# Raw loads interleaved with weight pairs, weight passes moved into a unit's levels, six copies for eight, and a second queue for two units' x

## The chip, the cores and the metric

The kernel runs on one core of a Trainium2 chip. The metric is device time in microseconds. Inputs and outputs lie in HBM. The five engines are PE (TensorE), DVE (VectorE), ACT (ScalarE), POOL (GpSimd) and SP (SyncE), which issues most of the DMAs.

## The reference

An attention-like recurrence over 768 tokens, for 4 batches of 8 heads of 48 columns, and then an MLP over the 3072 tokens:

```python
f = 1.0 / (1.0 + np.exp(-f_logit))
for t in range(S):
    state = f[:, :, t, :, None] * state + np.einsum('bhd,bhe->bhde', k[:, :, t], v[:, :, t])
    y[:, :, t] = np.einsum('bhd,bhde->bhe', q[:, :, t], state)
x = y.transpose(0, 2, 1, 3).reshape(B * S, H * D)      # 3072 x 384
h = x @ w_in                                           # 384 x 2048
out = (h * (1.0 / (1.0 + np.exp(-1.702 * h)))) @ w_out # 2048 x 384
```

The weights are given as 64-bit floats, the rest as 32-bit floats.

## The kernel before

**Units.** The tokens are cut into 12 units of 256 (`NALL`), three to a batch. A unit's attention (`attention(n)`) is a list of parts. First, f, q and k are loaded raw (`load_raw`, three tensors j = 0, 1, 2 for f, q, k) and turned so that the head's columns lie on partitions (`turn`: on PE for units 0 and 1, on DVE's stream transpose, L354, from unit 2 on). Then six levels of a scan follow. At each level the products of f over a stretch (`tot`, POOL, L425) are multiplied into X, which holds q and k (`promote`, DVE, L528 or L532), half of X is set aside on ACT (`set_aside`: Kc, L503, and Qc, L509), PE forms scores (`score`, L434), and DVE and ACT move them from PSUM to the matrix A (`evacuate`, L475, L494, L484). In units 2 and on, two levels share one score tile, `sc`, of which there is one. A later tile of it waits until the earlier one has been moved to A. A and v give y (`add`, L543), k and v give the chunk states (L652, DVE L676/L677), and states and q are added into y (L698).

**From y to x.** Part "W" copies y from PSUM to `yT` on ACT (L712: for each head of a pair, two directions f and two groups g, 48 partitions x 256 elements, so eight copies a unit), and `to_x` moves `yT` to `xT` in six DMAs, three a head (L762 the large one, L767 the two rests). Unit 11 has its own copy of this, `whole`.

**MLP.** `xT` is what the MLP multiplies: h = x w_in in blocks of 128 columns (`mlp_h`, L1110; three matmuls a block) and o = g w_out (`mlp_o`, L1124), for units 0 and 1 block by block as the weights come in. From unit 2 on it uses products of sums of the weights (L878, L1016).

**Weights.** The 64-bit weights come in 16 pairs of blocks of 128 (`pairs`: for each four blocks two of w_in, then two of w_out). A pair is fetched by SP into one of three buffers `bits` (`fetch_weights`, L208; two DMAs for w_in, one for w_out). It is then turned into 32-bit floats: a pass on ACT (L239) and three on DVE (L235, L228, and the add at L238). `convert()` emits the next of the three DVE operations, and the ACT pass with the first. When a pair is done, `fetch_weights` issues the next fetch. So where `convert()` stands in the program also decides where the next fetch stands in SP's queue. Pair 4, 5, 8, 9, 12 and 13 are w_in's for blocks 4 to 7, 8 to 11 and 12 to 15; 6, 7, 10, 11, 14 and 15 are w_out's.

**Order.** Up to the end of unit 2's attention the order on each engine is that of the program text (`manual_schedule`). `opening()` emits unit 0; `follow(n, fill, plan)` emits the parts of units 1 and 2. After each part it emits so many MLP items (`fill`), so many `convert()` and so many other operations (`chores`), by the table `PLAN`. An MLP item waits in the list until the pairs that it needs have been emitted. `parts_of(n)` lists a unit's parts, with the turns of unit n+1 (`begin_f`, `begin`, `begin_k`, `begin_gates`) between them, and with the loads of the raw tensors, each of which has one buffer. SP, ACT, DVE and PE each work their list in order.

In before, unit 1's second part issues all three raw loads of unit 2, and unit 2's turns each issue the raw load of unit 3 right behind them:

```python
second = parts[1][1]
parts[1] = parts[1][0], lambda: (second(), [load_raw(n + 1, j) for j in range(3)])
```

Of the kernel before, what the change touches and what calls it, by code (L numbers as in the profile page):

```python
# [23 lines left out]
def kernel(  # L24
# [33 lines left out]
    nc = tc.nc  # L58
# [6 lines left out]
    U = 256  # L65
# [190 lines left out]
            fetch_weights()  # L256


    def load_raw(n, j, engines=(nc.sync,)):
        if n >= NALL:  # L260
            return
        b, s0 = n // NU, n % NU * U
        src = (f_logit, q, k)[j]
        first = s0 - (j == 1)

        def span(head, token, dims, d=0):
            return bass.AP(src.tensor, src.offset + ((b * H + head) * S + token) * D + d, dims)
        if n < N_FILL:
            for a in range(NP):
                engine = engines[a * len(engines) // NP]  # L270
                to = by_pair[j][32 * a:32 * (a + 1), :, :R * D]
                if first < 0 and a == 0:

                    for r, rows in ((1, 16), (17, 15)):
                        engine.dma_start(
                            out=to[r:r + rows], in_=span(0, r * R - 1, [[R * D, rows], [S * D, 2], [1, R * D]])
                        )
                    engine.dma_start(out=to[:1, :, D:], in_=span(0, 0, [[R * D, 1], [S * D, 2], [1, (R - 1) * D]]))
                else:
                    engine.dma_start(out=to, in_=span(2 * a, first, [[R * D, 32], [S * D, 2], [1, R * D]]))  # L280
            return
        for f in (1, 0):
            for r in range(4):
                lo = 32 * (r % 2)
                width = R4 * D - lo
                part = span(r // 2, first + (0 if f else HALF), [[R4 * D, 32], [2 * S * D, NP], [1, width]], lo)
                nc.sync.dma_start(out=by_half[32 * r:32 * (r + 1), j, f, :, :width], in_=part)  # L287
            if f and first < 0:
                for r in range(4):
                    lo = 32 * (r % 2)  # L290
                    nc.sync.dma_start(
                        out=by_half[32 * r:32 * r + 1, j, f, :, :D - lo],
                        in_=q[b - 1, r // 2::2, S - 1:S, lo:].rearrange("a t d -> t a d"),
                    )
# [25 lines left out]
    def rows(h):  # L320
        return slice(h * HS, h * HS + D)
# [6 lines left out]
    def attention(n):  # L328
# [58 lines left out]
        def begin_f(pieces=None):  # L387
            def decay():
                turn(0, lambda f: F[:, ORDER.index(f) * SLOT:(ORDER.index(f) + 1) * SLOT], sigmoid, pieces)
            if n > N_FILL + 1 and "moved" in copied:  # L390
                with tc.issue_after(copied["moved"].ins):
                    decay()
            else:
                decay()
            if n >= N_FILL:
                load_raw(n + 1, 0)

        def begin():
            turn(1, lambda f: slot(query(n, f)))
            if n >= N_FILL or (n == 1 and 1 == 0):  # L400
                load_raw(n + 1, 1)

        def begin_k(between=None):
            turn(2, lambda f: slot((KR, KF)[f]))
            if n >= N_FILL or (n == 1 and 2 == 0):
                load_raw(n + 1, 2)
            if n >= N_FILL:
                set_aside(0, True)
                rest = between and between()
                promote(0)  # L410
                if rest:
                    rest()
            else:
                set_aside(0)
# [34 lines left out]
        def columns(h, g):  # L449

            return rows(h ^ g)
# [84 lines left out]
        def add():  # L536


            t["py"] = ps.tile([P, NG, NP, 2, HS], F32, tag="y", name=f"y_{n}")
            for a in range(NP):  # L540
                for f in (1, 0):
                    for h, g in TILES:
                        nc.tensor.matmul(  # L543
                            t["py"][columns(h, g), g, a, f, :],
                            lhsT=vts[n][g * HS:(g + 1) * HS, f, (2 * a + h) * D:(2 * a + h + 1) * D],
                            rhs=A[g * HS:(g + 1) * HS, h * NP + a, f, :],
                            start=(f == 1 and a == 0), stop=False, skip_group_check=True,
                        )
# [9 lines left out]
        def levels(l):  # L558

            scores()  # L560
            score(0, l, queries_aside(l))
            score(1, l + 1, queries(l + 1))
            promote(l + 1, l + 2 < NL)
            if l + 2 < NL:
                promote(l + 2)
            evacuate(l, l + 1)
            if l == 2:
                reverse_v(n)
# [71 lines left out]
        def _():  # L640
# [17 lines left out]
            if not n:  # L658
# [2 lines left out]

                seen = t["py"][HS:HS + 1, 1, 0, 1, :1]
                nc.scalar.copy(seen, seen)
            load_v(n + 1)
            st = att.tile([P, NC, NP, D], F32, tag="st", name=f"st_{n}", bufs=2)
            D64 = t["tms"][NL].rearrange("p (f a g) -> p f g a", f=2, a=NP)
            prev = t["ahead"] = last.get("st")
# [13 lines left out]
        def _():  # L681
# [24 lines left out]
            xT = mlp.tile([P, NK, width(n)], F32, tag="xT", name=f"xT_{n}", bufs=3)  # L706

            def half(h):
                for f in (1, 0):
                    for g in range(NG):  # L710
                        at, step = (g * HS, 1) if f else (U - 1 - g * HS, -1)
                        nc.scalar.copy(view(yT[rows(h)], at, [[U, NP], [step, HS]]), py[columns(h, g), g, :, f, :])  # L712
                to_x(lambda h: (yT[rows(h), :NK], lambda r, d: yT[r:r + d, NK]), xT[:, :, :U], NG, (h,))
            half(0)
            if n > N_FILL and n < NALL - 1:
                xTs[n] = xT
# [38 lines left out]
            xTs[n] = xT  # L755
            sums_of_x(n)

        def to_x(y, x, ng, hs=range(2)):

            for h in hs:  # L760
                most, rest = y(h)
                nc.sync.dma_start(out=x[h * D:(h + 1) * D].rearrange("p c (g t) -> p c g t", g=ng), in_=most)  # L762
                at = 0
                while at < D:
                    c, p = (h * D + at) // DR, (h * D + at) % DR
                    w = min(D - at, DR - p)
                    nc.sync.dma_start(  # L767
                        out=x[D2 + p:D2 + p + w, c].rearrange("p (g t) -> p g t", g=ng), in_=rest(h * HS + at, w)
                    )
                    at += w  # L770
# [419 lines left out]
    def parts_of(n):  # L1190

        parts = list(units[n][1])
        _, inter = parts.pop()
        if n and n != N_FILL:
            kind, scores = parts[0]
            _, ahead = units[n - 1][1][-1]
            def both():
                rest = ahead()
                scores()
                if rest:  # L1200
                    rest()
            parts[0] = kind, both
        if n + 1 < NALL:
            begin_f, begin, begin_k, begin_gates = units[n + 1][0]
            i = len(parts)
            if n + 1 < N_FILL:

                parts.append(("K", lambda: (begin_k(), begin_gates())))
                kind, head = parts[0]
                parts[0] = kind, lambda: (head(), load_raw(n + 1, 1), keep_up(1))  # L1210
                parts.insert(4, ("B", lambda: (begin(), load_raw(n + 1, 2))))
                parts.insert(2, ("B", begin_f))
            else:
                kind, states = parts.pop()
                if n in CARRY:
                    parts += [("B", begin_f), ("B2", begin), ("S1", lambda: (states(), begin_gates())), ("K3", begin_k)]
                elif n < N_FILL:
                    second = parts[1][1]
                    parts[1] = parts[1][0], lambda: (second(), [load_raw(n + 1, j) for j in range(3)])
                    def own():  # L1220
                        rest = inter()
                        rest()
                    parts += [(kind, states), ("W", own), ("B", begin_f), ("B", begin), ("B", lambda: (begin_gates(), begin_k()))]
                else:
                    parts += [("B", begin_k), (kind, lambda: (states(), begin_gates()))]
                    parts.insert(i - 3, ("B", lambda: (begin_f(), begin())))
        else:
            parts.append(("W", inter))
        return parts
# [53 lines left out]
    def opening():  # L1283
# [44 lines left out]
        for _ in range(NOP):  # L1328
# [4 lines left out]
    WAITS = {(1, "W", 1): 3}  # L1333
    PLAN = {
# [4 lines left out]
    }  # L1339
    fill += mlp_blocks((0, 0)) + mlp_blocks((0, 1))  # L1340
    fill += mlp_blocks((1, 0), (1, 1)) + mlp_blocks((0, 2), (1, 2)) + mlp_blocks((0, 3), (1, 3))
# [53 lines left out]
```

## Time and profile before

| | us |
|---|---|
| median of 3 runs (596.13 to 596.91) | 596.39 |
| the profiled execution | 596.8 |
| its span | 595.0 |
| PE busy | 568.3 (96%) |
| DVE busy | 435.8 (73%) |
| ACT busy | 299.6 (50%) |
| POOL busy | 136.2 (23%) |
| mean granted TensorE clock | 0.991 |

The span is what the profile covers; the profiled execution's own time is 1.8 us longer. All times inside a profile count from the span's start. In a line of a time line, the first number is the start, the second the time from the first to the last of the merged instructions, then engine, line, operation, output and inputs, the shape and the number of instructions; the bracket tells how long the engine was idle before it and which instruction ended that. PE shows each 32-bit matmul as two passes, so an h block of three matmuls is "x6" and an o matmul is "x2". SPq and ACTq are DMA issues on the queues of SP and ACT. The table by windows gives the busy time of each engine, then the granted TensorE clock, the busy share of the DMA engines and GB/s.

### The profile page before, as it was taken

The page shows a single profiled execution, that of the slowest core. Times are in us where ns is not written, and L with a number is a line of the kernel's source. Part 1 is how long each engine was busy: PE and PEld are TensorE (multiplying, and loading weights), DVE is VectorE, ACT ScalarE, POOL GpSimd, SP SyncE. Part 2 cuts the span into 40 slices and gives each one's busy share as a digit, 9 for nine tenths or more (in the row PEclk, how much of TensorE's full clock was granted, in tenths as well). Part 3 has the DMA queues.
Part 4 walks back from the last instruction along what each step waited for, and adds up shares of the span by engine and source line. Part 5 has one row for each costly group of instructions (what it writes and reads, how often), then busy time and mean ns, then how long its engine had stood idle before and what let it go on. Part 6 is the DMA issues. An engine that isn't in the chain of part 4 may idle for free.

```text
span 595.0 us, 18527 instructions
## 1 busy us (share of the span) xinstructions
PE 568.3 (96%) x7832; PEld 517.2 (87%) x7832; DVE 435.8 (73%) x697; ACT 299.6 (50%) x610; POOL 136.2 (23%) x226
## 2 busy tenths in 40 slices
PE   7989887899999999999999999999999999999997
PEld 6756574667789999999999999999999999998896
DVE  2897568985979778798787797786887786461284
ACT  4765534324452575474474574563663564552440
POOL 3020020145226610610600700700600602203000
PEclk9989899999999999999999999999999999999999
DMA  6868977434452443343452243453352121001000
GB/s 181 192 164 200 225 193 173 134 78 95 122 143 66 128 107 84 94 123 92 120 141 55 76 115 88 123 139 63 96 146 55 45 55 29 29 2 27 28 1 28
DMA packets 86772, 60.34 MB, mean 101 GB/s; under 512 B 33505, under 2 KB 78465, under 8 KB 86689
## 3 DMA queue, kind: packets, MB, share of 16 engines
q1 hardware_dynamic: 86352, 58.76, 39.4%
q8 instruction: 62, 1.02, 0.7%
q10 hardware_dynamic: 337, 0.39, 0.3%
q14 instruction: 21, 0.17, 0.1%
HBM read 45.49 MB, written 8.91 MB: 91 GB/s over the span
## 4 chain that ended last, share of the span: by engine, by line
PE 79%; DVE 8%; DMA 5%; issue 3%; ACT 2%; SPq 2%; DVEq 0%; ACTq 0%
PE h L1016 16%; PE o_Y L878 13%; PE o_Z L878 9%; PE h L1110 9%; PE h_y L1016 6%; PE sc L434 5%; PE o_X L878 5%; PE o L1124 4%; PE o_W L878 4%; DMA bits<-in_moe_w_in_dram 3%; PE y L698 2%; PE y L543 2%; PE sc L652 2%; DMA raw<-in_f_logit_dram 2%; SPq L287 1%
## 5 line engine op out<-in xcount | busy, mean ns | idle before, releaser
L532 DVE TENSOR_TENSOR X<-X,tot 128x1024 f32<-128x1024 f32 x50 | 65.6, 1313 | 42.7 <-PE sc L434 36.4
L503 ACT COPY Kc<-X 128x512 f32<-128x512 f32 x72 | 48.3, 670 | 71.6 <-DVE X L532 59.9
L978 POOL TENSOR_TENSOR E<-xT 128x128 f32<-128x128 f32 (+1 forms) x36 | 18.6, 528 | 235.0 <-DMA xT<-yT 204.4
L1110 PE MATMUL h<-xT,w_in 128*128 128x256 f32 x288 | 66.9, 388 | 4.8 <-DVE w_in L238 2.5
L1110 PEld LDWEIGHTS h<-xT,w_in 128*128 128x128 f32 x288 | 54.9, 193 | 15.1 <-issue 3.4
L1016 PE MATMUL h<-E,w_in 128*128 128x128 f32 (+1 forms) x476 | 62.5, 277 | 0.3 <-DVE g L1044 0.3
L1016 PEld LDWEIGHTS h<-E,w_in 128*128 128x128 f32 x476 | 57.3, 192 | 1.0 <-issue 0.5
L878 PE MATMUL o_Y<-T,S 128*128 128x192 f32 x320 | 57.6, 329 | 0.0
L1046 ACT ACTIVATE g<-g 128x512 f32<-128x512 f32 (+1 forms) x70 | 40.4, 590 | 26.6 <-DVE g L1044 26.6
L878 PEld LDWEIGHTS o_Y<-T,S 128*128 128x128 f32 x320 | 52.3, 190 | 0.5
L1044 DVE TENSOR_TENSOR g<-g,h 128x512 f32<-128x512 f32 (+1 forms) x58 | 36.1, 638 | 15.1 <-PE h L1016 14.1
L712 ACT COPY yT<-y 48x256 f32<-48x256 f32 x88 | 32.3, 367 | 28.8 <-PE y L698 27.8
L1124 PE MATMUL o<-w_out,g 128*128 128x384 f32 x128 | 45.4, 503 | 0.1
L354 DVE STREAM_TRANSPOSE X<-raw 128x512 f32<-128x512 f32 x40 | 42.3, 1116 | 3.1 <-PE y L698 2.7
L494 DVE COPY_PREDICATED A<-masks,sc 128x256 f32<-128x256 uint32 (+1 forms) x98 | 42.0, 504 | 0.0
L1124 PEld LDWEIGHTS o<-w_out,g 128*128 128x128 f32 x128 | 24.2, 195 | 15.5 <-issue 1.9
L1035 ACT ACTIVATE g<-h 128x512 f32<-128x512 f32 (+1 forms) x52 | 28.5, 576 | 10.0 <-PE h L1016 9.7
L1114 ACT ACTIVATE g<-h 128x256 f32<-128x256 f32 x48 | 17.8, 384 | 30.4 <-PE h L1110 30.3
L434 PE MATMUL sc<-X,Kc 48*64 48x64 f32 x1344 | 28.4, 221 | 3.8 <-ACT Kc L503 2.2
L434 PEld LDWEIGHTS sc<-X,Kc 48*64 48x64 f32 x1344 | 24.2, 135 | 8.0 <-ACT Kc L503 4.2
L878 PE MATMUL o_X<-w_out,g 128*128 128x192 f32 x160 | 29.9, 332 | 0.5 <-ACT o_X L842 0.5
L878 PE MATMUL o_W<-T,g 128*128 128x192 f32 x160 | 29.5, 331 | 0.0
(161 smaller groups left out, 1171.4 us busy)
## 6 DMA issues: line engine op xcount, KB each, us to landing
bits<-in_moe_w_out_dram SPq DMA_DIRECT2D x8, 768.0 KB, 5.4
raw<-in_f_logit_dram SPq DMA_DIRECT2D x48, 96.0 KB, 2.4
raw<-in_k_dram SPq DMA_DIRECT2D x48, 96.0 KB, 3.3
bits<-in_moe_w_in_dram SPq DMA_DIRECT2D x8, 576.0 KB, 6.7
raw<-in_q_dram SPq DMA_DIRECT2D x44, 96.0 KB, 2.2
k_tok<-z SPq DMA_DIRECT2D x64, 64.0 KB, 1.7
kt<-k_tok SPq DMA_DIRECT2D x16, 256.0 KB, 3.4
out_dram<-osb SPq DMA_DIRECT2D x20, 192.0 KB, 1.9
```

Source lines behind the costliest of these rows:

```text
L354: nc.vector.transpose(view(out, at, [[HALF, NP], [step, R4], [R4 * step, 32]]), by_half[:, j, f].rearrange("p a (j d) -> p (a j) d", j=R4) ...
L434: nc.tensor.matmul(t["sc"][h][g * HS:(g + 1) * HS, a, s, :], lhsT=t["Kc", l][rows(h), x:x + HS], rhs=rhs(h, a, g), start=True, stop=True,)
L494: moved = nc.vector.copy_predicated(out=view(A, c * HALF + at, dims), mask=mask.bitcast(U32), data=got)
L503: nc.scalar.copy(c.rearrange("p (n two m) -> p n two m", two=2, m=m), view(X, KF * SLOT, [[2 * m, SLOT // (2 * m)], [(KR - KF) * SLOT + m, ...
L532: nc.vector.tensor_tensor(x, x, y, ALU.mult)
L712: nc.scalar.copy(view(yT[rows(h)], at, [[U, NP], [step, HS]]), py[columns(h, g), g, :, f, :])
L878: nc.tensor.matmul(t[name], lhsT=lhs(f), rhs=rhs(f), start=(new and i == 0), stop=(i == HF - 1), skip_group_check=True,)
L1016: nc.tensor.matmul(ph[:, t], lhsT=WA[a][:, f * P:(f + 1) * P], rhs=E[n][b], start=(root and t == 0), stop=not goes_on, skip_group_check=True,)
L1044: nc.vector.tensor_tensor(to, to, part, ALU.add if sign > 0 else ALU.subtract)
L1046: nc.scalar.activation(to, to, AF.Gelu_apprx_sigmoid)
L1110: nc.tensor.matmul(ph, lhsT=w_in[:, c, ff * P:(ff + 1) * P], rhs=xTs[n][:, c, :], start=(c == 0), stop=(c == NK - 1))
L1124: nc.tensor.matmul(t["po"], lhsT=g[ff // FG][:, ff % FG, tt * P:(tt + 1) * P], rhs=w_out[:, ff, :], start=(ff == ffs[0]), stop=(ff == ffs[ ...
```

## The change

- Raw loads of unit 2: f behind unit 1's second part as before, q behind its fourth, k behind its fifth. Pair 6 thereby stands between f and q on SP, and pair 7 between q and k.
- Raw loads of unit 3: no longer behind unit 2's turns but in unit 2's own parts: f ahead of the second part, q behind it, k behind the third. The fetches of pairs 12, 13 and 14 stand ahead of all of them on SP, that of pair 15 between f and q.
- v of unit 2 is loaded by a later part (`begin`) of unit 1.
- `HOLES`: seven `convert()` are emitted inside unit 2's levels: three between setting aside level 0 and its multiplication, two, one and one ahead of later ones. `PLAN` emits fewer elsewhere and other numbers of MLP items in unit 1.
- In `half`, one copy over 112 partitions takes both heads of group 0; group 1 is copied as before. That makes four copies in the first half, two in the second. So that the 16 partitions between the heads hold something, `add` multiplies with 64 columns of v rather than 48 for the first head of group 0. Unit 11 keeps eight copies.
- For units 0 and 1, the three DMAs of the second head's x are issued by ACT, SP and ACT in turn, not by SP alone.

```diff
+    HOLES = {(N_FILL, 0): 3, (N_FILL, 1): 2, (N_FILL, 2): 1, (N_FILL, 4): 1}
+    def convert_in(n, l):
+        for _ in range(HOLES.get((n, l), 0)):
+            convert()
...
             if n >= N_FILL:
                 set_aside(0, True)
                 rest = between and between()
+                convert_in(n, 0)
                 promote(0)
...
+                        to, w = (slice(0, HS), HS) if h == g == 0 else (columns(h, g), D)
                         nc.tensor.matmul(
-                            t["py"][columns(h, g), g, a, f, :],
-                            lhsT=vts[n][g * HS:(g + 1) * HS, f, (2 * a + h) * D:(2 * a + h + 1) * D],
+                            t["py"][to, g, a, f, :],
+                            lhsT=vts[n][g * HS:(g + 1) * HS, f, (2 * a + h) * D:(2 * a + h) * D + w],
...
             score(1, l + 1, queries(l + 1))
+            convert_in(n, l + 1)
             promote(l + 1, l + 2 < NL)
             if l + 2 < NL:
+                convert_in(n, l + 2)
                 promote(l + 2)
...
-            load_v(n + 1)
+            if n != N_FILL - 1:
+                load_v(n + 1)
...
             def half(h):
-                for f in (1, 0):
-                    for g in range(NG):
+                for g in range(h, NG):
+                    for f in (1, 0):
                         at, step = (g * HS, 1) if f else (U - 1 - g * HS, -1)
-                        nc.scalar.copy(view(yT[rows(h)], at, [[U, NP], [step, HS]]), py[columns(h, g), g, :, f, :])
-                to_x(lambda h: (yT[rows(h), :NK], lambda r, d: yT[r:r + d, NK]), xT[:, :, :U], NG, (h,))
+                        to, of = (rows(h), columns(h, g)) if g else (slice(0, HS + D),) * 2
+                        nc.scalar.copy(view(yT[to], at, [[U, NP], [step, HS]]), py[of, g, :, f, :])
+                two = (nc.scalar, nc.sync) if h and n < N_FILL else (nc.sync,)
+                to_x(lambda h: (yT[rows(h), :NK], lambda r, d: yT[r:r + d, NK]), xT[:, :, :U], NG, (h,), two)
...
                 elif n < N_FILL:
-                    second = parts[1][1]
-                    parts[1] = parts[1][0], lambda: (second(), [load_raw(n + 1, j) for j in range(3)])
+                    def followed(i, *loads):
+                        kind, fn = parts[i]
+                        parts[i] = kind, lambda: (fn(), [load() for load in loads])
+                    for i, j in ((1, 0), (3, 1), (4, 2)):
+                        followed(i, lambda j=j: load_raw(n + 1, j))
...
-                    parts += [(kind, states), ("W", own), ("B", begin_f), ("B", begin), ("B", lambda: (begin_gates(), begin_k()))]
+                    parts += [(kind, states), ("W", own), ("B", begin_f), ("B", lambda: (begin(), load_v(n + 1))), ("B", lambda: (begin_gates(), begin_k()))]
                 else:
...
+                    second, third = parts[1][1], parts[2][1]
+                    parts[1] = parts[1][0], lambda: (load_raw(n + 1, 0), second(), load_raw(n + 1, 1))
+                    parts[2] = parts[2][0], lambda: (third(), load_raw(n + 1, 2))
...
-        1: ((0, 6, 2), (1, 1, 13), (2, 3, 0), (8, 4, 6), (16, 0, 11), (7, 0, 0), (0, 4, 0), (1, 0, 5), (6, 2, 0), (8, 6, 6),
+        1: ((0, 6, 2), (1, 1, 13), (2, 3, 0), (8, 4, 6), (3, 2, 0), (0, 0, 0), (0, 2, 0), (1, 2, 0), (1, 3, 0), (8, 4, 0),
             (3, 0, 1), (3, 0, 0), (2, 0, 0)),
-        2: ((8, 6, 0), (6, 7, 1), (14, 4, 0), (0, 0, 3), (5, 1, 10), (11, 2, 0), (0, 1, 6), (7, 6, 3)),
+        2: ((8, 2, 0), (6, 3, 1), (14, 6, 0), (0, 0, 3), (5, 0, 10), (11, 0, 0), (0, 0, 6), (7, 0, 3)),
```

More of the change, by code (lines that the diff above doesn't have):

```diff
@@ L394, in begin_f @@
                 decay()
-            if n >= N_FILL:
+            if n > N_FILL:
                 load_raw(n + 1, 0)
@@ L399, in begin @@
             turn(1, lambda f: slot(query(n, f)))
-            if n >= N_FILL or (n == 1 and 1 == 0):
+            if n > N_FILL:
                 load_raw(n + 1, 1)
@@ L404, in begin_k @@
             turn(2, lambda f: slot((KR, KF)[f]))
-            if n >= N_FILL or (n == 1 and 2 == 0):
+            if n > N_FILL:
                 load_raw(n + 1, 2)
@@ L756, in whole, with to_x @@
             sums_of_x(n)
-        def to_x(y, x, ng, hs=range(2)):
+        def to_x(y, x, ng, hs=range(2), queues=(nc.sync,)):
             for h in hs:
                 most, rest = y(h)
-                nc.sync.dma_start(out=x[h * D:(h + 1) * D].rearrange("p c (g t) -> p c g t", g=ng), in_=most)
+                engines = [queues[i % len(queues)] for i in range(3)]
+                engines.pop(0).dma_start(out=x[h * D:(h + 1) * D].rearrange("p c (g t) -> p c g t", g=ng), in_=most)
                 at = 0
@@ L766, in to_x @@
                     w = min(D - at, DR - p)
-                    nc.sync.dma_start(
+                    engines.pop(0).dma_start(
                         out=x[D2 + p:D2 + p + w, c].rearrange("p (g t) -> p g t", g=ng), in_=rest(h * HS + at, w)
```

## The prediction

> **What bounds the kernel now.** I read the page first, then PE's time line, SP's issue time line and the chain of waits. The page says that PE is busy for 568.3 of 595.0 us, and shows where the rest is.
>
> ```profile
> PE   7989887899999999999999999999999999999997
> PEclk9989899999999999999999999999999999999999
> ```
>
> Slices are 14.9 us. From slice 8 (119 us) on PE is full, so a microsecond won ahead of that point reaches the end if nothing behind it gives it back. All edits but one act ahead of 160 us. PE's time line shows what is lost there:
>
> ```profile
> 63.19 0.68 PE L652 MATMUL sc<-vt,kn 64*64 64x48 f32 x32 [1.37 <-ACT kn L605]
> 64.86 2.82 PE L1110 MATMUL h<-xT,w_in 128*128 128x256 f32 x6 [0.99 <-issue]
> ...
> 76.04 9.30 PE L1110 MATMUL h<-xT,w_in 128*128 128x256 f32 x42 [1.30 <-issue]
> ...
> 101.86 0.69 PE L434 MATMUL sc<-Qc,Kc 48*64 48x64 f32 x32 [3.42 <-DVE A L494]
> ...
> 108.98 10.22 PE L1110 MATMUL h<-xT,w_in 128*128 128x256 f32 x46 [1.77 <-DVE w_in L238]
> ```
>
> The last bracket is the idle time before the line and what ended it. I add up the work between 56.32 and 108.98 at full pace: h 1.33 us a block of three matmuls (10.22 for 46 passes), o 0.665 a matmul (6.65 for 20 passes), sc 1.09 a pair of levels, tkn 1.1, both y 1.04, sc of the states 0.93. That gives 37.7 us; the stage takes 52.7. So 15 us is the most that this stage can return. The chain of waits names a cause at both ends of it:
>
> ```profile
> 56.68 5.06 DMA bits<-in_moe_w_out_dram
> 61.76 0.90 ACT bits L239
> 62.66 0.48 ACT kn L605
> ...
> 98.35 7.60 DMA bits<-in_moe_w_in_dram
> ```
>
> Weight pairs land late because SP's single queue sends three blocks of raw loads ahead of them:
>
> ```profile
> 40.51 7.18 SPq L287 DMA_DIRECT2D raw<-in_f_logit_dram  x8
> 47.82 4.59 SPq L287 DMA_DIRECT2D raw<-in_q_dram  x8
> 52.52 4.07 SPq L287 DMA_DIRECT2D raw<-in_k_dram  x8
> 56.68 0.90 SPq L208 DMA_DIRECT2D bits<-in_moe_w_out_dram  x2
> ```
>
> The same is seen again at 77.09 to 96.85 (raw of unit 3) ahead of pairs 12 and 13, whose second one lands at 105.95. PE's h at 108.98 waits for pair 13's conversion (108.92).
>
> **Part 1: unit 2's raw loads, pairs 6 and 7 between them.** SP's order becomes f, pair 6, q, pair 7, k, pairs 8, 9, 10, then xT. It reaches f about 0.85 us sooner, since two of xT's six DMAs leave it (0.6 each in L762/L767's rows). Pair 6 is issued at 47.0, behind f. A w_out pair takes 5.4 us to land (page part 6), up to 7.8 in the rows of bits; I take 6.2, since f lies ahead: 53.2. Q's last DMA needs pair 6's queue slot (each SP transfer waits for the one eight before it in the instruction list), so pair 7 goes at 54.2 and lands at 59.6; k's last needs that slot, so pair 8 goes at 60.0 and lands at 66 (w_in: 6.5 to 6.7). Level 5's chain does not suffer: pair 6 is wanted on ACT at 54.
>
> What is queued behind the new waits counts more. ACT now holds, in this order, both kn copies, pair 7's pass, one gelu, pair 8's pass, one gelu, the yT copies. The kn copies are free at 57.5, so the 1.37 us stall goes; pair 5's last pass on DVE moves ahead of level 5's multiplications, which wait for PE (57.09), so the 0.75 us wait at 58.79 goes. But yT now waits for pair 8: 66.0 + 0.90 (pass) + 0.7 (gelu and dispatch) = 67.6, against 69.21 before. PE reaches that point near 64 and waits. Gain in yT: 1.6 us.
>
> **Part 2: six copies, two queues.** Copies cost 0.38 each (3.03 for 8, at 48 rows; a row of 112 partitions is not in the trace. I take the same time for the same 256 elements a row; the dearest neighbour, twice as long, would eat the gain). Before: 69.21 to h's start at 76.04 is 6.83. After: six copies 2.3, then ACT's own issue and landing of the 48x768 DMA (73.28 to 76.04 before: 2.76) makes 5.1, so h of unit 1 starts at 72.7, 3.3 us sooner. Two issues on ACT cost 0.43 to 0.69 each in ACT's queue rows of the opening; they delay pair 9's pass, which F's and X's transposes follow on DVE (end 80.0, before 82.31), so they are covered. In unit 0 they push Kc at 36.05 by 0.45 us; xT is there 1.8 sooner; nothing of this survives, as pairs 6 to 8 gate what follows. The 64-column weight loads add nothing: 64 passes already move 64 columns each in 1.04.
>
> The Trainium skill (DMA: Bandwidth & Descriptors, "Issuing engines are not separate DMA queues") says that transfers started by several engines share the same 16 DMA engines, and only issue time is saved. By that rule the second queue is worth one issue, 0.6, and the start would be the same 72.7 here, as I count no bandwidth; if pair 10's bytes still fill the engines, it would be about 74.
>
> **Part 3: passes in holes.** Unit 2's block: eight h blocks 72.7 to 83.3 (h_7 now ahead of sc), then sc. Kc_0 follows the gelu of h_5 (80.7): 81.1 to 82.5 with Qc. In before, X's multiplication followed at once (84.56 behind 84.48). Now pair 10's pass on ACT (0.90), its shift (0.55) and its add (0.95) come between, as X's line stands behind them on DVE: +2.4. So X runs 85.05 to 86.3, Kc_1 to 87.0; the second half of sc waits on PE from 84.0 to 87.0, 3.0 us against 0.57. This hole is not hidden; it is the dearest piece of the change. Next level: pair 11's pass and shift put X at 89.1, Qc_2 ends 91.6, X 92.9, A's three rows (0.68 + 1.31) 94.9. PE's o blocks end at 93.0, so sc_18 waits till 94.9; before, 93.21. So far the whole gain is lost (-1.7).
>
> Then it turns. Before, six passes stood on DVE between 92.87 and 96.63, and sc_19 waited 3.42 for A. After, X starts at 96.05, one add, Kc/Qc, X to 99.85, A to 101.15: sc_19 at 101.2 (before 101.86). Behind it pair 13 landed long ago (issued at 84, once pair 10's buffer is free, landing near 90): shuffle 0.58, two passes 1.1, a sum 0.5, add 0.96: 104.2. PE arrives at 104.05 after 4 o and 2 h passes. So h goes on at 104.2 against 108.98: **-4.8**.
>
> **Behind that.** DVE holds the same work after this point in both programs; T's sums now come before F's transposes, and pair 15's shift waits for its ACT pass at 115. I find slack left: st ends at 138 where PE wants it at 141; sc_22 has about 1 us. Unit 3's raw q and k are issued later (97 to 106), needed at 119 and 127. I charge 0.3 of those bounds (0 to 1.5). Eight later units save two copies, 0.75 us of ACT each; PE's waits there are 1.9 us on DVE's g in all, so 0 to -1, taken -0.2.
>
> Sum: profiled time 596.8 (span 595.0 and 1.8 around it) - 4.8 + 0.3 - 0.2 = 592.1. That execution is 0.4 above the median of 596.39; I give 592.
>
> **Rivals.** The instruction lists of both programs show every edit in place, so that it does not happen is none. (a) *Slower: pair 8 holds yT.* Pairs 6, 7 and 8 land one after another through the slots of q and k. With 7.8 us each (the longest row) instead of 5.4 to 6.6, they land at 54.8, 63.0 and 71.5; yT starts at 73.1, h at 78.2, and the walk above ends at 109.7: +0.7, and with one more long PE wait in it about +2.5: 599. It decides from a landing of 70.8 on. For it: eight slots, SP waiting 4.0 + 2.9 us for bits in this stage; against it: 307 GB/s moved at 60 to 66.
> (b) *Given back.* The holes' 3.0 and 1.9 us come in full and sc_19 has no gain, because DVE's T sums or pair 15 make PE wait: 596, no change.
> (c) *More.* The holes' X lines start at the transposes' end (80.0) as the gelus run ahead, and the later stalls shrink: 589.
> (d) *The clock.* In before, the 3.42 us of idle time is followed by a low granted clock:
>
> ```profile
> 100.00:102.00 2.00, 0.14 (x9) 0.17 (x12) 2.00 (x7) 1.00 (x2) 0.00 (x0) 1.00 1.05 239
> 102.00:104.00 2.00, 2.00 (x65) 1.62 (x64) 1.66 (x4) 0.93 (x1) 0.00 (x0) 0.64 1.04 263
> 104.00:106.00 2.00, 2.00 (x5) 1.04 (x4) 1.38 (x2) 0.00 (x0) 0.00 (x0) 0.51 1.04 271
> ```
>
> The clock is the third number from the end; about 3.4 us at half pace cost 1.7. The 1.30 and 1.77 us waits had no such tail. Mine of 3.0 may have it: at 88 it is hidden, since o would then end at 94.7, before 94.9. If it comes after sc_18 it adds 1.7: 593.8. The Trainium skill (TensorE: Matmul & The Clock Gate, Part 1) says that an idle window of about 3.4 us halves the clock, in free-running windows. The trace agrees in size.
>
> **Numbers.** Forecast with (d)'s two outcomes 0.62 (590 to 594.5), (c) 0.10, (b) 0.11, (a) 0.17. A measurement of this kernel tells about 0.2% (1.2 us) from no change: faster means under 595.2, slower over 597.6. Faster 0.72, same 0.11, slower 0.17. The range leaves out most of (a) and the far end of (c): 589 to 597.4.
>
> **What would show it.** Right: kn with no DMA wait ahead of it; unit 1's h start between 72 and 74; a PE wait of about 3 us before the second half of sc of unit 2; none over 1 us at h of blocks 8 to 11; pair 13 landed by 95. Wrong: yT starting after 70 behind pair 8, X's first multiplication at once behind Qc_0, or new PE waits between 110 and 160.

## The result, and the profile after

| | before | after |
|---|---|---|
| median of 20 runs each, us | 597.04 (596.13 to 600.37) | 594.91 (592.77 to 597.54) |
| ratio after/before, 95% interval | | 0.9955 (0.9943 to 0.9967) |
| the profiled execution, us | 596.8 | 595.5 |
| its span | 595.0 | 593.2 |
| PE busy | 568.3 | 568.8 |
| ACT busy | 299.6 | 288.4 |
| mean granted TensorE clock | 0.991 | 0.991 |

The change makes the kernel faster by 0.45%, 2.7 us by the ratio (the medians differ by 2.1 us). The forecast was 592.0 us, with a range of 589 to 597.4, so sign and range held. The gain was about half of the 4.4 us forecast by the medians and three fifths by the ratio, and 594.9 lies just outside the 590 to 594.5 that had the chance of 0.62. In the two profiled executions the difference is 1.3 us, where the sum of the prediction had 4.7.

The page of after, for the two rows that were read first in before:

```profile
PE   7979888999999999999999999999999999999997
PEclk9989988999999999999999999999999999999999
```

PE is full from slice 7 on (before: slice 8). The clock row has its 8s in slices 2, 5 and 6 (before: 2 and 4); slice 5 is 74 to 89 us. PE's time line of after for the same stage:

```profile
61.71 1.12 PE L663 MATMUL sc<-vt,kn 64*64 64x48 f32 x64
63.18 1.45 PE L1125 MATMUL h<-xT,w_in 128*128 128x256 f32 x6 [0.35 <-issue]
...
73.51 0.70 PE L1125 MATMUL h<-xT,w_in 128*128 128x256 f32 x2 [1.49 <-DMA xT<-yT]
74.42 11.88 PE L1125 MATMUL h<-xT,w_in 128*128 128x256 f32 x46 [0.21 <-DVE w_in L238]
...
89.71 0.70 PE L442 MATMUL sc<-X,Kc 48*64 48x64 f32 x32 [2.78 <-ACT Kc L511]
...
97.34 0.70 PE L442 MATMUL sc<-Qc,Kc 48*64 48x64 f32 x32 [1.57 <-DVE A L502]
...
98.43 5.83 PE L1139 MATMUL o<-w_out,g 128*128 128x384 f32 x12
104.19 0.70 PE L442 MATMUL sc<-Qc,Kc 48*64 48x64 f32 x32
...
106.67 10.52 PE L1125 MATMUL h<-xT,w_in 128*128 128x256 f32 x48
```

Three of the waits shown of before are gone: 1.37 us for kn, 3.42 us for A and 1.77 us for the weights. Unit 1's h starts at 73.51 instead of 76.04. In their place stand 2.78 us for Kc, in the first hole, and 1.57 us for A. Two lines are too long for their work: 46 passes of h take 11.88 us (10.22 in before), and 12 of o take 5.83 us (4.14 in before). The table by windows says why; the clock is the third number from the end:

```profile
74.00:76.00 2.00, 1.79 (x5) 1.30 (x5) 2.00 (x4) 0.00 (x0) 0.00 (x0) 0.67 0.88 324
76.00:78.00 2.00, 2.00 (x6) 1.54 (x5) 2.00 (x3) 1.15 (x2) 0.00 (x0) 0.50 1.06 310
...
98.00:100.00 2.00, 2.00 (x38) 1.33 (x30) 1.41 (x3) 0.06 (x1) 0.00 (x0) 0.64 0.78 116
100.00:102.00 2.00, 2.00 (x4) 1.09 (x4) 1.55 (x2) 1.08 (x2) 0.00 (x0) 0.51 0.98 379
```

The clock is at half (0.50) from 74.7 to 78.1 and from 98.6 to 102.0, and once more from 37.1 to 40.5. The profiled execution of before has as many such stretches (37.7 to 41.1, 65.0 to 68.4, 102.6 to 106.0), so the mean clock is 0.991 in both. They don't all cost the same. In before, the one at 102.6 lies ahead of the 1.77 us for pair 13, and the chain of waits comes to pair 13 by DVE and SP, not by PE, so it cost nothing. What the one at 65.0 cost is not shown: an h block took 2.82 us in it (1.45 in after), y stands behind that block, and yT's first copy waits for y:

```profile
69.21 3.03 ACT L712 COPY yT<-y 48x256 f32<-48x256 f32 x8 [0.31 <-PE y L698]
```

In after, the one at 74.7 lies ahead of the chain of holes. The two profiled executions also hide a difference. Over all runs the mean clock is 0.990 in before (the 71 runs beside the experiments) and 0.994 in the full change (26 runs), so the change has about one stretch fewer as a rule.

The gain along the way, at points with the same work done ahead of them: 1.9 us at the third pass of h of block 8 (107.10 against 108.98), 2.0 us at 128.23 against 130.24, and 1.3 us at the last o_Z (587.12 against 588.40). The spans differ by 1.8 us, but the time around the span grew from 1.8 to 2.2 us, in every run of after (2.14 to 2.30), so the last matmul is the better mark.

### The profile page after: what moved, and what is told of

The parts are those of the page before. It is cut to its first block, busy times and chain, and to the rows that moved or that the text cites. A ratio compares the mean times of both kernels' runs of the same rounds, so it can differ in the third digit from the quotient of the medians.

```text
span 593.2 us, 18507 instructions
## 1 busy us (share of the span) xinstructions
PE 568.8 (96%) x7832; PEld 518.0 (87%) x7832; DVE 438.1 (74%) x697; ACT 288.4 (49%) x588; POOL 139.2 (23%) x226
## 4 chain that ended last, share of the span: by engine, by line
PE 83%; DVE 6%; ACT 5%; DMA 3%; issue 2%; ACTq 1%; SPq 0%; DVEq 0%
PE h L1031 16%; PE o_Y L893 13%; PE h L1125 10%; PE o_Z L893 9%; PE sc L442 6%; PE h_y L1031 6%; PE o L1139 6%; PE o_X L893 5%; PE o_W L893 4%; DMA bits<-in_moe_w_in_dram 2%; PE y L710 2%; PE y L552 2%; PE sc L663 2%; DVE X L540 1%; DVE g L1059 1%
## 5 line engine op out<-in xcount | busy, mean ns | idle before, releaser
L540 DVE TENSOR_TENSOR X<-X,tot 128x1024 f32<-128x1024 f32 x50 | 67.6, 1351 | 39.7 <-PE sc L442 31.4
L993 POOL TENSOR_TENSOR E<-xT 128x128 f32<-128x128 f32 (+1 forms) x36 | 16.0, 453 | 227.3 <-DMA xT<-yT 227.3
L725 ACT COPY yT<-y 48x256 f32<-48x256 f32 (+1 forms) x66 | 21.1, 369 | 29.2 <-PE y L710 28.8
L388 POOL TENSOR_SCALAR F<-F 128x1024 f32<-128x1024 f32 x10 | 12.9, 1286 | 81.0 <-ACT F L391 81.0
```

The costliest lines, as they stand in the source:

```text
L540: nc.vector.tensor_tensor(x, x, y, ALU.mult)
```

## The experiments

All were timed in five rounds beside runs of the kernel before, four kernels to a comparison, with six to twelve runs of each. Medians of before were 597.63, 598.1 and 597.9 us in the three comparisons, so ratios are compared, not times.

| kernel | median, us | ratio to before (95%) |
|---|---|---|
| copies and second queue alone | 597.05 | 0.9993 (0.9972 to 1.0015) |
| loads and holes alone | 595.29 | 0.9972 (0.9950 to 0.9993) |
| first hole behind F | 594.11 | 0.9941 (0.9920 to 0.9962) |
| unit 2's loads together again | 597.66 | 1.0003 (0.9987 to 1.0019) |
| pair 8's pass behind yT | 598.55 | 1.0017 (1.0003 to 1.0031) |
| idle matmuls | 593.88 | 0.9938 (0.9919 to 0.9957) |
| one queue | 596.35 | 0.9983 (0.9966 to 0.9999) |
| first hole behind F, and idle matmuls | 594.51 | 0.9952 (0.9930 to 0.9974) |
| the full change again | 594.88 | 0.9950 (0.9937 to 0.9962) |
| second queue in unit 0 only | 595.31 | 0.9956 (0.9940 to 0.9972) |
| second queue in unit 1 only | 597.0 | 0.9978 (0.9964 to 0.9992) |
| idle matmuls again | 594.19 | 0.9934 (0.9911 to 0.9956) |

**The change in its parts.** First, before with the six copies, the 64 columns and the second queue only (the hunks in `add`, `half` and `to_x` of the diff above):

> The kernel before with only the six copies (and the 64 columns of v they need) and the second queue. My theory: unit 1's h starts about 1.8 us sooner (74.2, not 76.04), but the stage still ends with the second of pairs 12 and 13 landing at about 106 and its conversion at 108.9, so the time stays: 597.0, -0.4 to +0.4 against before. Rival (the copies and the queue carry the gain): -1.5 to -2.2.

Measured: ratio 0.9993, no difference; the interval reaches as far as -1.7 us, so the weak end of the rival isn't excluded. In its profile unit 1's h starts at 76.82, later than before and not sooner (the clock is at half from 64.3 to 71.1 in this execution), and the old waits are still there (3.42 us for A at 103.43, 1.94 us for w_in at 110.79). Then the reverse, the full change with these three hunks undone:

> The changed kernel with the eight copies and the single queue of before. My theory: yT still starts at 68.4 behind pair 8's pass, unit 1's h starts 1.5 to 1.8 us later (75.2), and everything behind it to the h blocks 8 to 11 hangs on that start, so the whole 1.6 us is lost: 596.4, -0.4 to -0.8 against before. Rival (the order of loads and passes carries the gain alone): -2 or better against before, as the full change.

Measured: 0.9972, between the two theories. Loads and holes bring something by themselves, 1.7 us, and about 1 us less than the full change; the intervals overlap. h of unit 1 starts at 75.28.

Then the order of the loads alone undone, with the holes, copies and queue in place:

```diff
-                    for i, j in ((1, 0), (3, 1), (4, 2)):
+                    for i, j in ((1, 0), (1, 1), (1, 2)):
```

> The changed kernel with unit 2's three raw loads together again, ahead of pairs 6 and 7. My theory: pair 6 lands near 62 and ACT holds its pass ahead of the copies to A, so kn, the states and y come near 66 to 70, yT starts at about 71.5 and unit 1's h at 76: +2.5 against the full change, 597.4. Rival (it does not matter in which order these loads go, since pair 8 lands at the same time): 0 to +0.5 against the full change.

Measured: 1.0003; the whole gain is gone, as the theory said. ACT's time line of this kernel shows the old stop in its worst form:

```profile
61.47 0.91 ACT L239 ACTIVATE bits<-bits 128x768 f32<-128x768 f32 x1 [4.84 <-DMA bits<-in_moe_w_out_dram]
```

ACT stands 4.84 us before pair 6, kn comes at 64.05 and yT at 72.51 (68.36 in after). So without the interleaving of unit 2's loads nothing of the gain is left. The interleaving without the moved passes, and unit 3's loads by themselves, were not tried.

**The first hole.** The three conversions between Kc_0 and the first multiplication are taken out of the hole and emitted right behind F's part:

```diff
-    HOLES = {(N_FILL, 0): 3, (N_FILL, 1): 2, (N_FILL, 2): 1, (N_FILL, 4): 1}
+    HOLES = {(N_FILL, 1): 2, (N_FILL, 2): 1, (N_FILL, 4): 1}
...
-            (3, 0, 1), (3, 0, 0), (2, 0, 0)),
+            (3, 3, 1), (3, 0, 0), (2, 0, 0)),
```

> The changed kernel with the first hole's three operations (pair 10) emitted behind unit 2's F turn instead of between setting aside level 0 and its multiplication. My theory: X's first multiplication starts at 85.4 instead of 87.7, PE's 2.8 us wait ahead of the second half of the first scores falls under 0.7, and the next level starts 2.1 sooner: -2.1 against the full change, 592.8. Rival (the passes only move, DVE gives the same 2.4 us back at the transposes): 0 to -0.5 against the full change.

```profile
74.09 13.48 PE L1125 MATMUL h<-xT,w_in 128*128 128x256 f32 x48 [3.22 <-DMA xT<-yT]
...
88.77 0.70 PE L442 MATMUL sc<-X,Kc 48*64 48x64 f32 x32 [0.58 <-ACT Kc L511]
```

The wait fell from 2.78 to 0.58 us as expected, but the time only by 0.5 to 0.8 us by the ratios, and that is within the uncertainty (0.9941 against 0.9955 and 0.9950). In the profiled execution, 48 passes of h take 13.48 us instead of 10.5, because the clock is at half from 73.1 to 79.9, twice as long as in after. So h ends 1.3 us later than in after, and the next level still starts 0.9 us sooner (96.41 against 97.34): the hole gave its 2.2 us, and in this execution the clock took more than half of it back.

**Pair 8's pass.** In after, ACT waits 4.99 us for pair 8 and only then reaches the yT copies. Here its pass stands behind them:

```diff
-(1, 3, 0), (8, 4, 0),
+(1, 1, 0), (8, 6, 0),
```

> The full change with ACT's pass of pair 8 (landed at 67.2 us in the changed kernel, where it holds the yT copies until 68.4) written behind the yT copies in ACT's order. Theory (the landing of pair 8 is the term that was mis-sized, and yT sets unit 1's first layer): the yT copies start at about 65.7, the x of unit 1 lands at about 71.4 and the first layer starts at 71.5 instead of 73.5; pair 9's add at 73.5 then stops it at its fifth block (two blocks of 0.7 us and more are covered first), so about 0.9 us is left: 594.0 us at the median, ratio to the kernel before 0.9940. Rival (the hole chain of the second unit, which starts at Kc_0, sets the end and not the first layer of unit 1): no more than 0.3 us, 594.6 us, ratio 0.9950.

Measured: 1.0017, 3.7 to 4 us worse than the full change. Both theories fell. The copies did start earlier, at 66.60. SP's time line, and then PE's:

```profile
68.50 6.78 SPq L782 DMA_DIRECT2D xT<-yT  x3
```

```profile
74.25 0.67 PE L1125 MATMUL h<-xT,w_in 128*128 128x256 f32 x2 [2.41 <-DMA xT<-yT]
76.60 12.71 PE L1125 MATMUL h<-xT,w_in 128*128 128x256 f32 x46 [1.69 <-DVE F L361]
```

The first xT transfer was issued at 67.92, 1.8 us sooner than in after, and h still could not start before 74.25. The last of SP's three small transfers went out only at 74.7, after 5.0 us of waiting for an earlier piece of xT to land, and the third pass of h ran at 76.60 (74.42 in after). The rest of the loss is clock: it is at half from 74.9 to 81.8 and from 92.0 to 98.8, each time twice as long as in after. The fetches of pairs 8, 9 and 10 were issued at 59.7 to 63.7, ahead of xT. So xT's landing isn't set by when the copies end. Other traces fit this: in after, first hole behind F, both edits together, the full change again, unit 0 only and this one, the first transfer goes out between 67.92 and 69.68 us and h starts between 73.50 and 74.25, and the earliest issue has the latest start. The two idle-matmul profiles, which are later as a whole, have 70.9 and 71.1 us for the one and 74.9 and 75.2 for the other. That the weights' bytes ahead of xT hold it fits these times, but no run takes them away.

**The queue.** Three kernels differ from the full change in one expression:

```diff
-two = (nc.scalar, nc.sync) if h and n < N_FILL else (nc.sync,)
+two = (nc.sync,)                                               # one queue
+two = (nc.scalar, nc.sync) if h and n == 0 else (nc.sync,)     # unit 0 only
+two = (nc.scalar, nc.sync) if h and n == 1 else (nc.sync,)     # unit 1 only
```

> The full change with the three transfers from yT to xT of unit 1's second half all on SP's queue again. Theory (ACT's queue takes the second half's issue time off SP's: three issues of 0.6 us one after another become two beside one): unit 1's first layer starts 0.6 to 0.8 us later, and 0.6 to 0.8 us is lost at the end: 595.6 us at the median, ratio to the kernel before 0.9967. Rival (the last landing is set by the last xT copy and not by the queue, as the copies and queue by themselves gave nothing): within 0.2 us of the changed kernel, 594.9, ratio 0.9955.

Measured: 0.9983, 1.7 to 2 us behind the full change, more than either theory had. The expectation speaks of unit 1 alone, but the edit puts unit 0's x on SP's queue too, and the profile showed SP late already at 38.71, behind unit 0's x. So the next two kernels split the queue by unit:

> The full change once more, beside the three kernels below on the same chip, so that they can be compared with it. Both theories: a ratio to the kernel before of 0.9943 to 0.9967, as in the first comparison.

> The full change with the second queue in unit 0 alone; unit 1's x goes by SP's queue again. In the one-queue experiment SP came to the weights behind unit 0's x at 38.71 us instead of 36.90, to pair 8's at 63.58 instead of 60.51, and ACT's pass of pair 8 stood at 70.42 instead of 67.28. Theory (the queue's worth of 1.4 to 1.7 us lies in unit 0, where SP is free 1.8 us sooner and every later weight issue with it): pair 8's pass at 66.5 to 68.0, within 0.5 us of the full change. Rival (the worth lies in unit 1's x itself, whose last issue stands 1.2 us sooner): 1.0 to 1.6 us behind the full change.

> The full change with the second queue in unit 1 alone; unit 0's x goes by SP's queue again. Theory (the worth lies in unit 0): pairs 4 and 5 are issued behind unit 0's x at 38.2 to 38.7 instead of 36.9, pair 8's pass falls to 68.5 to 70.5, 1.0 to 1.6 us behind the full change. Rival (it lies in unit 1's x): within 0.4 us of the full change.

Measured: 0.9950 for the full change, 0.9956 with the queue in unit 0 only, 0.9978 in unit 1 only. The theory holds: what the second queue is worth lies in unit 0. There SP is done with x 1.3 to 2.2 us sooner (36.5 to 36.9 against 38.2 and 38.7). Pair 8 is issued at 59.43 (full change again), 59.85 (unit 0 only), 62.78 (unit 1 only) and 63.58 us (one queue). How the one leads to the other is not shown. The first load of f is issued at 40.38, 40.09 and 40.32 us in the first three, so the lead is gone there; it is back at pair 7 (54.03 and 53.59 against 56.14). And in the profiled execution of loads and holes alone, which has one queue, SP is done with x at 38.20 and pair 8 is still issued at 60.61. With the queue in unit 1 only, ACT's and PE's time lines show the price:

```profile
69.69 0.90 ACT L239 ACTIVATE bits<-bits 128x768 f32<-128x768 f32 x1 [7.62 <-DMA bits<-in_moe_w_in_dram]
```

```profile
70.90 5.18 PE L1139 MATMUL o<-w_out,g 128*128 128x384 f32 x10 [3.38 <-ACT g L1129]
76.07 10.93 PE L1125 MATMUL h<-xT,w_in 128*128 128x256 f32 x48
```

Pair 8's pass stands at 69.69 instead of 67.28 and holds the gelu ahead of yT, so o waits 3.38 us (0.72 in after); o's ten passes then fall into a half-clock stretch and take 5.18 us (3.49 in after), and unit 1's h starts at 76.07. This is the mechanism of rival (a) of the prediction, "pair 8 holds yT", though pair 8 landed before the 70.8 us from which (a) was to decide.

**The clock.** Idle matmuls, whose result nothing reads, are put where PE waited in after: two before unit 1's h, four between the two scores of level 0 of unit 2, two before level 1's.

```diff
+            if (n, l) == (N_FILL, 0):
+                keep_up(4)
...
+                if (n, ff) == (1, 0):
+                    keep_up(2)
...
-    WAITS = {(1, "W", 1): 3}
+    WAITS = {(1, "W", 1): 3, (2, "V", 1): 2}
```

> The full change with idle matmuls (their result is read by nothing) put where PE waited in the profile of the changed kernel: two before the first layer's first block of unit 1 (wait 1.49 us), four between the two score blocks of level 0 of the second half (wait 2.78 us), two before level 1's (wait 1.57 us). Theory (the half-clock stretches of 3.4 us at 74.4 and 98 follow these waits, and cost 1.6 and 0.6 us to 1.8 us each): granted clock at least 0.997, no half-clock stretch between 74 and 103, 592.8 to 593.3 us at the median, ratio to the kernel before 0.992. Rival (the clock falls at its own times, whatever PE does in waits of 1.5 us): clock as before, the idle matmuls cost up to 0.3 us where they run over the end of a wait, 595.0 to 595.5 us, ratio 0.9955 to 0.9965.

> The kernel with idle matmuls once more, directly beside the full change, as the version that is meant to beat both. In its first profile the first scores began 2.5 us late (16.1 us instead of 13.6, behind late first loads), and unit 1's later layers still began 0.7 us earlier than in the changed kernel. Theory (the half-clock stretches at 74 and 98 follow PE's waits and cost 1.6 to 2.2 us in the executions that have them): 1.0 to 2.0 us under the full change in this comparison, and no half-clock stretch between 70 and 104. Rival (the difference of the first comparison, 1.0 us, was the chip's spread): within 0.4 us of the full change.

PE's time line in the second run:

```profile
73.26 1.24 PE L116 MATMUL idle<-masks,ident 128*128 128x320 f32 x4
75.17 10.86 PE L1129 MATMUL h<-xT,w_in 128*128 128x256 f32 x48 [0.67 <-DMA xT<-yT]
...
95.32 1.24 PE L116 MATMUL idle<-masks,ident 128*128 128x320 f32 x4
97.10 0.69 PE L442 MATMUL sc<-Qc,Kc 48*64 48x64 f32 x32 [0.54 <-DVE A L502]
...
98.19 4.14 PE L1143 MATMUL o<-w_out,g 128*128 128x384 f32 x12
...
106.13 4.05 PE L1129 MATMUL h<-xT,w_in 128*128 128x256 f32 x18
```

At the place, the theory holds. Between 70 and 104 the granted clock is 1.00 in both profiles, o takes 4.14 us again, and from unit 1's first h to block 8's takes 31.0 us in both (33.2 in after, 32.5 in the full change again). The mean clock is 0.994 or more in each of the twelve runs and 0.998 over all of them (0.994 over the 26 of the full change). At the median, 1.0 and 0.7 us were gained over the full change of the same or the first comparison, half of what was expected; by the ratios 0.9938 and 0.9934 against 0.9955 and 0.9950, about as much as they are uncertain. In both profiles PE was later at 56 us, ahead of any edit, by 2.5 and 1.1 us (in the first one the first scores began at 16.1 us instead of 13.6); nothing found ties that to the edits. This version has the lowest ratio of all, 0.9934, but that it beats the full change isn't certain.

The traces show which waits have a half-clock stretch behind them. Up to the last matmuls, every stretch of the 14 traces lasts 3.41 us or twice that, and within a trace their starts are whole multiples of 3.41 us apart (37.12, 74.67 and 98.56 in after: 11 and 7 steps). So an execution can be cut into steps of 3.41 us. These are the steps of after that hold its three waits; the first number behind the comma is PE's busy time:

```profile
71.25:74.67 3.42, 1.72 (x6) 0.70 (x5) 1.84 (x4) 0.90 (x1) 0.00 (x0) 1.00 0.69 146
84.91:88.32 3.41, 2.02 (x39) 1.44 (x37) 2.03 (x3) 1.31 (x2) 0.00 (x0) 1.00 0.17 8
88.32:91.73 3.41, 2.02 (x36) 1.43 (x37) 1.80 (x4) 2.01 (x4) 0.00 (x0) 1.00 0.82 222
95.15:98.56 3.41, 1.84 (x67) 1.19 (x66) 2.85 (x6) 2.15 (x4) 0.00 (x0) 1.00 1.15 230
```

The waits of 1.49 and 1.57 us each lie within one step, in which PE was busy for 50% and 54%, and the next step runs at half. The wait of 2.78 us is spread over two steps with 59% in each, and neither has a stretch behind it. Counted over the 14 traces, from 20 to 585 us: of the steps at full clock, all 19 in which PE was busy for less than 44% were followed by one at half, none of the 2223 with 64% or more were, and 9 of the 39 between. PE's busy time is modelled, and between these two bounds it doesn't decide: the full change again has a step with 54%, at 94.9 us, and no stretch behind it. In both profiles with all eight idle matmuls, no step between 70 and 102 us is below 80%. Where the steps lie differs from one execution to the next, so whether a wait of 1.5 us has a stretch behind it is partly luck.

Both edits together:

> The full change with two edits: the second half's first hole, in which h_7 stood before Kc_0's pass, is moved behind F as in the experiment on the first hole (which gained 0.8 us against the changed kernel), and two idle matmuls stand before unit 1's first layer and two before level 1's scores. Theory (the wait before the second scores is gone by the first, the half-clock stretches by the second, and the two add up because the first gained only 0.8 of 2.1 us through a half-clock stretch at 74 to 80): wait before the second scores under 0.7 us, granted clock at least 0.997, 592.0 us at the median, ratio to the kernel before 0.9905. Rival (the clock doesn't follow these waits): 594.1 us, ratio 0.9941.

Measured: 0.9952, no better than either. The four idle matmuls in the hole were left out here; two waits of 1.3 us remained, at 85.65 and 87.68, and 16 passes of o behind them took 6.51 us instead of 5.43, at a mean clock of 0.85 from 88 to 98 (nearly all of both waits lies in the step from 84.1 to 87.6, in which PE was busy for 27%). The two gains don't add up.

## Why the prediction was right and where it was off

**Part 1, right, with one term too small.** kn has no DMA wait, the states at 61.71 follow without a stop, and pair 8 gates yT as said. Pair 8 was there at 67.2 us instead of 66.0: +1.2, and yT began at 68.36 instead of 67.6. Of that, 0.5 us is a later issue (60.51 instead of 60.0). The other 0.7 is a slip in the sum: the prediction counted 6.0 us from issue to landing, although it gives 6.5 to 6.7 for w_in beside it, and 6.7 is what it took. One wait was not foreseen: pair 5's last pass, moved ahead, now lets h wait 1.07 us at 55.47. It cost nothing, as pair 8 came later than PE.

**Part 2, right in its sum by some luck, wrong in one sentence.** From the first yT copy to h took 5.15 us (5.1 predicted). Its two terms were off in opposite directions: the copies took 1.96 us instead of 2.3 (over 112 partitions 0.38 and 0.40 us each, over 48 about 0.37), and from ACT's issue of the large piece to h it was 3.17 us instead of 2.76. In the seven other profiles with interleaved loads and six copies in which this h waits for xT, it took 5.32 to 7.65 us, so the sum met the shortest. The start of "about 74", which the prediction gave for the case that pair 10's bytes still fill the engines, is nearer to theirs (73.50 to 75.17) than 72.7.

The step that failed is "nothing of this survives, as pairs 6 to 8 gate what follows", said of unit 0's x. Pairs 6 to 8 are themselves queued behind unit 0's x on SP. The unit-1-only kernel, in which SP comes to the weights at 38.21 instead of 36.90, is 1.7 us slower at the end. The sum had the sooner loads in its Part 1, as 0.85 us at f (measured 0.3, as the four issues of pairs 4 and 5 took 3.11 us instead of 2.01) and the pair issues after it, but it didn't see that this, and not unit 1's x, is what the second queue buys. The Trainium skill (DMA: Bandwidth & Descriptors, "Issuing engines are not separate DMA queues") says that only issue time is saved. The traces can't tell its size in unit 1: yT to h takes 6.25 us by one queue (unit 0 only) and 5.73 us by two (the full change again), but up to 7.65 us by two elsewhere. In unit 0, 1.3 us of issue time was worth more than itself, by a way that stays open.

**Part 3, right in its waits.** 2.78 us before the second half of sc (3.0 predicted), the 3.42 us for A gone, pair 13's add at 105.51, ahead of its first use, and h of blocks 8 to 11 without a wait. Pair 13 was issued at 86.84 instead of 84; nothing waited for its landing, so that can't be read. None of the three signs of being wrong came: yT started before 70, X's multiplication stood 2.3 us behind Qc_0, and the profile shows no wait of PE between 110 and 160.

**The mis-sized terms.** Kc_0 came at 84.03 instead of 81.1, 2.9 us late. Of that, 0.8 us had come up by unit 1's start, 0.2 us more by waiting for pair 9's add, and 1.7 us because 46 passes of h took 11.88 us in the half-clock stretch at 74.7; 0.2 us is left over. That delay runs down the chain of holes: sc_18 at 97.34 instead of 94.9, sc_19 at 104.19 instead of 101.2 with the second stretch at 98, and h of block 8 2.9 us later than the -4.8 us of the forecast. So -4.8 became -1.9.

The term is rival (d). It was reasoned that "the 1.30 and 1.77 us waits had no such tail" and that only the new wait of 3.0 us might have one, which would be hidden. That is so of these two waits, but it passes over the stretch of before at 65.0, which stands behind waits of 1.37 and 0.99 us; in the step ahead of it PE was busy for 1.05 of 3.41 us. In after it was the other way round than forecast: the waits of 1.49 and 1.57 us were followed by a stretch, the one of 2.78 us was not. The stretches last 3.4 us, or twice that, as the window of 3.4 us in the Trainium skill (TensorE: Matmul & The Clock Gate, Part 1) would give. The Trainium skill's rule for what halves the clock, an idle window of that length, isn't what these traces show: steps in which PE was busy for half of the time sufficed.

**The base.** The forecast was counted down from a median of 3 runs, 596.39 us. Over 20 runs the median of before is 597.04, so 0.65 of the 2.9 us by which 592.0 was missed lies in the base.

**Behind that, too low.** 0.1 us was charged for everything after 109 us; 0.6 us was lost between there and the end, in pieces that were not followed up.

## What to carry to other kernels

When weights and activations share one issuing queue, look at what stands behind each transfer in it: moving two small transfers off SP's queue near 36 us was worth more than moving the same two near 71 us, where the wait was. A transfer that is issued earlier need not land earlier, so find out what bounds its landing before making its source ready sooner. After a rewrite, place PE's remaining waits on the time line and look for half-clock stretches behind each of them, even behind waits of 1.5 us: PE's busy share of each 3.41 us told more here than the length of a wait. And compare clocks over many runs, as one profiled execution can have more stretches than most.

## What had not been expected of the hardware

Each half-clock stretch of 3.4 us takes 0.003 off the mean clock of a run, so the mean clock counts them: 0.997 is one, 0.994 two, 0.991 three. In the 20 runs of after, the median time is 593.5 us at 0.997 (8 runs), 595.0 at 0.994 (6) and 595.6 at 0.991 or less (6). So 2.1 us of the spread of this kernel, nearly 5 us, go with their number. But the six runs of the full change again have no such order (594.25 us at 0.991, 595.12 at 0.997), and runs of the idle-matmul kernel at a clock of 1.000 still lie between 591.8 and 596.5 us, so it is not the only cause; late first loads, as at 16.1 us above, may be another.

The time outside the span, 1.8 us in every run of before, has a mean of 2.2 us in after and in most kernels with interleaved loads, of 2.0 us in loads and holes alone and in one queue (from 1.8 to 2.2 there), and of 1.85 us with the loads together. Where it goes was not found.
